# The first loads of `a` issued ahead of ScalarE's function table, with a new order of the whole program

## The chip, the cores and the metric

The kernel runs on one core of a Trainium2 chip. The time is device microseconds of one execution of the program; a kernel's time is the median of its runs. Beside the timed runs there is one profiled execution, whose trace is what the views below are read from. In the trace PE is TensorE (its weight loads stand apart as PEld), DVE is VectorE, ACT is ScalarE, POOL is GpSimd and SP is SyncE, and a name with a q behind it (ACTq, SPq) is that engine's sequencer issuing a DMA.

## The reference

A gated linear recurrence over 768 positions for 4 x 8 heads of width 48, with a complex decay per position, followed by a two-layer network with a squared ReLU:

```python
mag = np.sqrt(a_re * a_re + a_im * a_im)
scale = np.minimum(mag, 0.999) / (mag + 1e-06)
a_re_n, a_im_n = (a_re * scale, a_im * scale)
for t in range(S):
    S_re, S_im = a[t] * S (complex) + k[t] v[t]^T (into S_re)
    y[:, :, t] = q[:, :, t] @ S_re
x = y as (4*768, 384)
h = x @ w_in                       # 384 -> 2048
g = np.maximum(h, 0.0) ** 2
out = g @ w_out                    # 2048 -> 384, float32
```

## The kernel before

The 3072 tokens are cut into six units of 512. Each unit n goes through the same stations. Its `a`, `q`, `k`, `v` are loaded (`load`). `chain` turns `a` into running products: square roots by Ln and Exp on ACT with products on DVE (`roots`, `raw_products`, `normalise`), then two PE transposes of the totals (L1162 with `perm`; in unit 0 `joint`, L1183), copies to `e` on ACT (L1194, L1197), a scan of small products on DVE (L1283 to L1353, which writes `xn`), two transposes back (L1162 with `ident`), and the application to q and k (`apply`, L1422 to L1450). `pairs` then takes the eight heads two at a time: scores on PE (L1589), masks on DVE (L1595), states on PE and DVE (L1619, L1634), mix on PE (L1647, L1651), a copy to `yt` on ACT (L1657) and DMAs into `xT` (L1665). `dense` multiplies `xT` by `w_in` (L1707), ACT applies the squared ReLU (L1739, L1740), and the second product follows (L1754 in unit 0, L1908 from unit 1 on, where sums of blocks replace one product in eight; L1800 and L1908 in the last unit). In unit 0 there is also the conversion of the weights: each of 16 pieces is fetched by POOL (L833), scaled by ACT (L846, L847) and put together on DVE (L849, L852).

All of this is a list of steps handed to a planner (`Plan`): each step has an engine, an assumed duration, what it reads and writes, and a rank. The planner runs a list schedule over the assumed durations: the engine that is free first takes, of its steps that are ready, the one with the lowest rank. The order in which they come out is the order of the instructions on each engine. While PE would stand idle in it, the planner puts in multiplications of the identity by itself (L751), which nothing reads. Ranks are made from the station and the unit, and then shifted by a table of numbers, for groups of steps and for single steps:

```python
rank = 100 * s[4][0] + s[4][1] + groups.get(g, 0) + single.get(n, 0)
...
n = min((n for n in wait[e] if at[n] <= t), key=lambda n: (steps[n][4], n))
```

In unit 0 the loads of `a` come in three parts for each of the real and the imaginary half: two of four heads' halves (z = 0) and one of the other four heads (z = 1). SP issues the real parts and ACT the imaginary ones:

```python
queue = pool if n or half else act if j else sp
```

The function table is asked for in the program's first lines, ahead of every planned step (L673), and two small negations that ACT makes for PE (L1141) and the squares of the real part (L992) come behind it on ACT. POOL issues the loads of q and k, of v and of the weights behind two copies (L945) that wait for the two halves of `a`.

Of the kernel before, what the change touches and what calls it, by code (L numbers as in the profile page):

```python
# [638 lines left out]
def fast_path(ctx, tc, q, k, v, a_re, a_im, moe_w_in, moe_w_out, out, flag, ots, blocks_of):  # L639
# [28 lines left out]
    dve, pool, act, sp = nc.vector, nc.gpsimd, nc.scalar, nc.sync  # L668
# [1 line left out]

    const = ctx.enter_context(tc.tile_pool(name="const", bufs=1))
    psum = ctx.enter_context(tc.tile_pool(name="psum", bufs=1, space=PSUM))
    act.preload_act_table_set("natural_log_exp_and_others")  # L673

    def sb(name, n, dtype=F32, rows=C):
        return const.tile([rows, n], dtype, name=name)
# [36 lines left out]
                                                           r=2, b=2)  # L713
# [41 lines left out]
    def vs(n):  # L755
        return n % 2 if n < ROOM else 0

    def tt(n):
        return n / 960.0 + 0.07
# [4 lines left out]
    def ac(n):  # L764
        return n / 1200.0 + 0.18
# [3 lines left out]
    def step(*args, **kw):  # L769
        return plan.add(*args, **kw)  # L770
# [4 lines left out]
    def dma(q, reads, writes, fn, rank, size, lat=1.8, group=None, dur=None):  # L775
        name, took = ("POOL", 0.67) if q is pool else ("SP", 0.62) if q is sp else ("ACT", 0.6)
        step(name, dur or took, reads, writes, fn, rank, (lat, size), group)

    CHAIN, PAIR, DENSE, CONV, LATE = 2, 1, 3, 3, 5
# [114 lines left out]
    def parts(n):  # L894

        t, got = n * L, []
        while t < (n + 1) * L:
            b, s = divmod(t, S)
            m = min(S - s, (n + 1) * L - t)
            got.append(((t - n * L) // W, m // W, b, s))  # L900
            t += m
        return got

    def spans(i):

        return ((0, C, 0),) if i % 2 == 0 else ((C // 2, C, 0), (0, C // 2, C // 2))

    def load(n):
        rank = (CHAIN, n)
        for half, name, pair in ((0, "a", (a_re, a_im)), (1, "qk", (q, k))):  # L910
            for z in range(2):
                t = aq[z][:, half * Z:(half + 1) * Z].rearrange(
                    "p (r h x) -> p r h x", r=2, h=HH)
                late = []
                if half and n == 1:
                    late = [("gate", 0)]
                if half and n > 2:
                    late = [("xT", (n - 1) % 2, NM - 1)]
                if half and n == 0:
                    late = [("gate",)]  # L920

                if n == 1 and half == 0:
                    late = [("gk", z)]
                    step("POOL", 0.3, [(k_, z, 1) for k_ in ("KC", "KC0", "KC1")], late,
                         lambda z=z: pool.tensor_copy(
                             out=gate[:, 0:W - 1], in_=KC[z].rearrange(
                                 "p (i y x) -> p i y x", i=W, x=KW)[:, 1:W, 1, 0]), rank)

                cut = 2 if n == 0 and half == 0 and z == 0 else 1
                for u in range(cut):  # L930
                    for j, ap in enumerate(pair):
                        for p0, m, b, s in parts(n):
                            hs = slice(u * HH // cut, (u + 1) * HH // cut)
                            src = ap[b, z * HH + hs.start:z * HH + hs.stop, s:s + m * W, :]
                            src = src.rearrange("h (p c) d -> p h (c d)", c=W)
                            queue = pool if n or half else act if j else sp
                            dma(queue, late,
                                [(name, z)] + ([(name, z, "r", j, u)] if n == 0 else []),
                                lambda t=t, p0=p0, m=m, j=j, src=src, queue=queue, hs=hs:
                                queue.dma_start(out=t[p0:p0 + m, j, hs], in_=src),  # L940
                                rank, m * 3072 // cut, 5.0 if n else 3.0, group=n)
            if n == 0 and half == 0:
                for z in range(2):
                    step("POOL", 0.2, [("a", z)], [("gate",)],
                         lambda z=z: pool.tensor_copy(out=gate[:, z:z + 1],  # L945
                                                      in_=aq[z][:, Z - 1:Z]), rank)
        t = vv[vs(n)].rearrange("p (i h d) -> p i h d", i=W, h=H)
        for i in range(W):
            b, s = divmod(n * L + i * C, S)
            vrank = (CHAIN, 1) if n == 1 else (DENSE, 6 + n)  # L950
            for lo, hi, at in spans(i):
                src = v[b, :, s + at:s + at + hi - lo, :].rearrange("h p d -> p h d")
                dma(pool, [("gate", 0)] * (n == 1) + [
                    ("xT", (n - (vs(n) == vs(n - 1))) % 2, NM - 1)] if n else [("gate",)],
                    [("v", vs(n))], lambda i=i, lo=lo, hi=hi, src=src: pool.dma_start(
                        out=t[lo:hi, i], in_=src), vrank, (hi - lo) * 1536, 4.0, group=n)

    def chain(n):
        rank = (CHAIN, n)
# [15 lines left out]
        def roots(z):  # L975
# [5 lines left out]
            cut = 2 if n == 0 and z == 0 else 1  # L981
            size = Y // cut
            for u in range(cut):
                def k(*js, u=u):
                    return key(z, *js) if n else [("f", z, j, u) for j in js]
# [2 lines left out]
                    return x[:, ts(u, size)]  # L988
                if n == 0:

                    step("ACT", ac(size), [("a", z, "r", 0, u)], k(0),
                         lambda u=u: act.activation(  # L992
                             out=part(f0, u), in_=A[z][:, ts(u, size)], func=AF.Square), first)

                    def square(u=u):
                        x = A[z][:, Y + u * size:Y + (u + 1) * size]
                        dve.tensor_tensor(out=part(f1, u), in0=x, in1=x, op=ALU.mult)
                    step("DVE", tt(size), [("a", z, "r", 1, u)], k(1), square, first)
# [138 lines left out]
        K = [(k_, 0, q_) for k_ in ("KC", "KC0", "KC1") for q_ in range(2)]  # L1137
        nperm, minus = (yts[i][:, 0:C] for i in range(2))
        if n == 0:
            for i, by in ((1, ident), (0, perm)):  # L1140
                step("ACT", 0.25, [], [("yt", i)], lambda i=i, by=by: act.mul(  # L1141
                    out=yts[i][:, 0:C], in_=by, mul=-1.0), rank)
            for z in range(2):
                roots(z)
                raw_products(z)
# [914 lines left out]
    for n in range(AFTER):  # L2060
        for j in range(3):
# [1 line left out]
    verdict()  # L2063

    plan.shift(
        groups={11: -1.01, 12: 6.22, 13: 0.95, 15: 438.73, 16: 438.73, 17: -235.2, 20: 1.52, 72:
# [5 lines left out]
        single={19: -99.45, 23: -302.38, 32: 6.69, 37: 19.99, 41: 15.87, 42: 425.47, 44: 16.14, 67:  # L2072
# [14 lines left out]
    with tc.manual_schedule():  # L2087
        got = plan.emit(flag[0:1, 0:1])
    return got
# [59 lines left out]
```

## Time and profile before

| what | us |
|---|---|
| three runs, median (lowest to highest) | 656.53 (653.69 to 657.35) |
| profiled execution, whole | 657.09 |
| its span, first to last instruction | 655.3 |
| PE busy in the span | 641.8 (98%) |
| DVE busy | 574.8 (88%) |
| ACT busy | 379.3 (58%) |
| POOL busy | 150.0 (23%) |

The 657.09 of the profiled execution hold its span and 1.8 us around it. Busy time counts the filling multiplications too (L751, 45.5 us, nearly all in the first 60 us), so PE's share says little about the beginning; there the chain of work that ended last runs over DVE, and later over PE.

### The profile page before, as it was taken

How to read it: one execution, taken by the hardware profiler on the slowest of the kernel's cores; microseconds unless marked ns; L12 is line 12 of the kernel's file. 1: busy time of each engine (PE TensorE's matmuls, PEld its weight loads, DVE VectorE, ACT ScalarE, POOL GpSimd, SP SyncE). 2: the span in 40 equal slices, each digit the busy share in tenths (PEclk: the TensorE clock that was granted, in tenths of full speed). 3: DMA queues.
4: the chain of work that ended last, by engine and by line, in shares of the span. 5: the costliest groups of instructions: out<-in, count | busy, mean ns of one | idle time of the engine just before them, and what ended most of it. 6: DMA issues, size and time to landing. Idle time of an engine off the chain costs nothing.

```text
span 655.3 us, 13462 instructions
## 1 busy us (share of the span) xinstructions
PE 641.8 (98%) x5064; PEld 576.7 (88%) x5064; DVE 574.8 (88%) x1188; ACT 379.3 (58%) x651; POOL 150.0 (23%) x258
## 2 busy tenths in 40 slices
PE   8989999999999999999999999999999999999996
PEld 8978887687778988998989998989999989988996
DVE  6999999999799999988998997996978999379991
ACT  6999589975656356457356648057558164145500
POOL 7311543232200031042052052130050210022110
PEclk9999999999999999999999999999999999999999
DMA  6951679147810146433175344174270152258541
GB/s 208 352 165 43 149 181 303 33 106 186 222 49 2 37 109 147 108 96 99 48 176 130 80 113 97 27 196 115 52 181 26 38 143 62 62 198 262 191 169 31
DMA packets 34631, 81.80 MB, mean 125 GB/s; under 512 B 7894, under 2 KB 13411, under 8 KB 34556
## 3 DMA queue, kind: packets, MB, share of 16 engines
q0 software_dynamic: 17024, 58.60, 31.9%
q1 hardware_dynamic: 15356, 20.04, 11.9%
q10 hardware_dynamic: 2176, 2.20, 1.2%
q8 instruction: 42, 0.69, 0.5%
q14 instruction: 33, 0.27, 0.1%
HBM read 48.76 MB, written 4.72 MB: 82 GB/s over the span
## 4 chain that ended last, share of the span: by engine, by line
PE 69%; DVE 19%; DMA 5%; issue 3%; ACT 2%; SPq 1%; POOL 0%; DVEq 0%; ACTq 0%; POOLq 0%
PE d L1908 26%; PE d L1707 24%; PE sc L1589 3%; PE yp L1647 2%; PE d L1800 2%; PE d L1754 2%; PE yp L1651 2%; DVE f L1450 2%; PE tr L1619 2%; DMA aq<-in_a_im_dram 2%; PE tr L1800 2%; DVE f L1422 1%; PE sc L1800 1%; DMA e<-xn 1%; DMA xT<-yt 1%
## 5 line engine op out<-in xcount | busy, mean ns | idle before, releaser
L1707 PE MATMUL d<-xT,w 128*128 128x256 f32 x912 | 204.6, 380 | 0.7 <-DMA xT<-yt 0.6
L1707 PEld LDWEIGHTS d<-xT,w 128*128 128x128 f32 x912 | 171.4, 190 | 25.4 <-DMA xT<-yt 1.0
L1908 PE MATMUL d<-w,g 128*128 128x192 f32 x576 | 99.7, 326 | 0.0
L1739 ACT ACTIVATE g<-d 128x512 f32<-128x512 f32 x76 | 45.1, 594 | 87.6 <-PE d L1707 85.7
L1908 PEld LDWEIGHTS d<-w,g 128*128 128x128 f32 x576 | 94.5, 190 | 0.6
L1908 PE MATMUL d<-T,g 128*128 128x192 f32 x432 | 78.0, 329 | 0.3 <-DVE g L1922 0.3
L1908 PEld LDWEIGHTS d<-T,g 128*128 128x128 f32 x432 | 70.9, 190 | 1.9 <-DVE g L1922 0.8
L1864 POOL DMA_DIRECT2D out_dram<-ot x22 | 12.8, 580 | 202.3 <-DVE ot L1931 163.4
L1922 DVE TENSOR_TENSOR g<-g 128x512 f32<-128x512 f32 x72 | 48.5, 686 | 9.2 <-PE d L1908 4.6
L1496 POOL DMA_DIRECT2D KC<-f x56 | 34.7, 625 | 77.9 <-issue 44.8
L1740 ACT ACTIVATE g<-g 128x512 f32<-128x512 f32 x80 | 50.5, 632 | 2.6
L1539 ACT COPY QT<-aq 32x512 f32<-32x512 f32 x57 | 35.3, 619 | 23.7 <-DVE aq L1536 23.0
L1536 DVE STREAM_TRANSPOSE aq<-f 128x768 f32<-128x768 f32 x40 | 47.9, 1272 | 0.2
L1657 ACT COPY yt<-yp 112x512 f32<-112x512 f32 x24 | 26.6, 1107 | 36.1 <-PE yp L1651 36.1
L751 PEld LDWEIGHTS d<-ident 128*128 128x128 f32 x366 | 44.7, 202 | 3.1 <-POOL ident masks.py:199 1.6
L751 PE MATMUL d<-ident 128*128 128x128 f32 x366 | 45.5, 287 | 1.6 <-POOL ident masks.py:199 1.6
L1450 DVE TENSOR_TENSOR f<-aq 128x768 f32<-128x768 f32 (+1 forms) x56 | 44.3, 838 | 0.5
L1754 PE MATMUL d<-w,g 128*128 128x384 f32 x128 | 43.8, 490 | 0.0
L1589 PEld LDWEIGHTS sc<-QT 96*64 96x64 f32 x736 | 34.6, 137 | 3.5 <-issue 2.5
L1589 PE MATMUL sc<-QT 96*64 96x128 f32 (+1 forms) x736 | 36.8, 251 | 0.8 <-DVE A L1595 0.7
L1754 PEld LDWEIGHTS d<-w,g 128*128 128x128 f32 x128 | 23.8, 190 | 14.6 <-issue 0.4
L1931 DVE TENSOR_TENSOR ot<-ot,d 128x192 f32<-128x192 f32 x70 | 23.6, 349 | 14.4 <-PE d L1908 10.8
(274 smaller groups left out, 1170.6 us busy)
## 6 DMA issues: line engine op xcount, KB each, us to landing
QT<-aq SPq DMA_DIRECT2D x152, 64.0 KB
f<-in_moe_w_in_dram POOLq DMA_DIRECT2D x8, 768.0 KB, 6.1
f<-in_moe_w_out_dram POOLq DMA_DIRECT2D x8, 768.0 KB, 4.9
out_dram<-ot POOLq DMA_DIRECT2D x22, 192.0 KB, 2.2
KC<-f POOLq DMA_DIRECT2D x20, 192.0 KB, 4.4
xT<-yt SPq DMA_DIRECT2D x36, 96.0 KB
aq<-in_q_dram POOLq DMA_DIRECT2D x8, 384.0 KB, 5.4
aq<-in_k_dram POOLq DMA_DIRECT2D x8, 384.0 KB, 6.3
```

Of the source, the lines that this page charges most:

```text
L751: plan = Plan(lambda b: pe.matmul(bank[b][:, 0:C], lhsT=ident, rhs=ident, start=True, stop=True), ["d2", "d1", "d0"], lambda ap: tc.nc.val ...
L1450: lambda j=j, r=r, o=o: dve.tensor_tensor(out=o[:, :, :, r * D:(r + 1) * D], in0=qk[:, j], in1=a[:, r], op=ALU.mult), late[z])
L1496: lambda i=i, queue=queue, lo=lo, hi=hi, a0=a0, a1=a1: queue.dma_start(out=kc[lo:hi, i], in_=nat[a0:a1]),
L1536: lambda nat=nat, dst=dst, j=j: dve.transpose(out=dst[:, j], in_=nat), rank)
L1539: lambda b=b, t=t, T6=T6: act.copy(out=t[32 * b:32 * b + 32, b], in_=T6[32 * b:32 * b + 32, i % 2, b]),
L1589: pe.matmul(sa[r:r + C // 2, j, :, lo:32], lhsT=T[:, j, 1, h, ts(late, C // 2)], rhs=T[:, j, 0, h].rearrange("p (c t) -> p c t", c=W)[:, : ...
L1707: pe.matmul(ps, lhsT=w1[:, f // FP, m, ts(f % FP, C)], rhs=xT[:, n % 2, m, ts(grp, G)], start=(m == 0), stop=(m == NM - 1))
L1739: act.activation(out=o, in_=ps, func=AF.Relu)
L1740: act.activation(out=o, in_=o, func=AF.Square)
L1754: pe.matmul(ps, lhsT=gt[:, f % 2, ts(i, C)], rhs=w2[:, f], start=(f == 0), stop=(f == NF - 1))
L1908: pe.matmul(bank[b][:, 0:DH], lhsT=gs(r, h)[:, j - 4 * h], rhs=w(j), start=first and j == 0, stop=last and j == NT - 1)
L1922: step("DVE", tt(4 * C), gk(x0, h) + gk(x1, h), gk(o, h), lambda: dve.tensor_tensor(out=gs(o, h), in0=gs(x0, h), in1=gs(x1, h), op=op), (0 ...
```

## The change

The table load leaves the program's head and becomes a planned step of ACT with an assumed 1.28 us; the two negations and the squares of unit 0 read its key, so they come behind it, and the loads of `a`, which do not read it, come ahead. The assumed time from the issue to the landing of the first parts of `a` (z = 0 and z = 1, real and imaginary) goes from 3.0 to 2.0 us. The table of shifts is another one: 38 groups and 92 single steps before, 30 and 77 after, with hardly a number in common. The order of all engines was worked out anew with it; apart from the filling multiplications, of which there are four fewer, both kernels hold the same instructions.

```diff
-    act.preload_act_table_set("natural_log_exp_and_others")
...
                                 queue.dma_start(out=t[p0:p0 + m, j, hs], in_=src),
-                                rank, m * 3072 // cut, 5.0 if n else 3.0, group=n)
+                                rank, m * 3072 // cut, 5.0 if n else 2.0 if half == 0 else 3.0,
+                                group=n)
...
-                    step("ACT", ac(size), [("a", z, "r", 0, u)], k(0),
+                    step("ACT", ac(size), [("a", z, "r", 0, u), ("table",)], k(0),
                          lambda u=u: act.activation(
                              out=part(f0, u), in_=A[z][:, ts(u, size)], func=AF.Square), first)
...
         if n == 0:
+            step("ACT", 1.28, [], [("table",)], lambda: act.preload_act_table_set(
+                "natural_log_exp_and_others"), (CHAIN, 0.001))
             for i, by in ((1, ident), (0, perm)):
-                step("ACT", 0.25, [], [("yt", i)], lambda i=i, by=by: act.mul(
+                step("ACT", 0.25, [("table",)], [("yt", i)], lambda i=i, by=by: act.mul(
                     out=yts[i][:, 0:C], in_=by, mul=-1.0), rank)
...
     plan.shift(
-        groups={11: -1.01, 12: 6.22, 13: 0.95, 15: 438.73, 16: 438.73, 17: -235.2, 20: 1.52, 72:
...
+        groups={4: -101.6, 15: 450.38, 16: 451.94, 19: -213.0, 30: -204.21, 97: -103.99, 108: 0.71,
...
```

In the rows of the order below, the lines of the new kernel stand one lower than before between L674 and L938, the same up to L1137, and two higher from L1143 on (L1164 is what L1162 was, L1597 what L1595 was); the numbers behind the names of tiles are one lower (those of `d` excepted). The banks are `d_64` to `d_66`, `sc`, `tr` and `yp`.

ScalarE's first instructions before:

```order
L673 ACT_TABLE_LOAD
L1141 ACTIVATE yt_98<-ident 128x128
L1141 ACTIVATE yt_97<-perm 128x128
L940 DMA aq_76<-in_a_im_dram 128x2x192 x2
L940 DMA aq_77<-in_a_im_dram 128x4x192
L992 ACTIVATE f_78<-aq_76 128x384 x2
```

and now:

```order
L939 DMA aq_75<-in_a_im_dram 128x2x192 x2
L939 DMA aq_76<-in_a_im_dram 128x4x192
L1140 ACT_TABLE_LOAD
L1143 ACTIVATE yt_97<-ident 128x128
L1143 ACTIVATE yt_96<-perm 128x128
L992 ACTIVATE f_77<-aq_75 128x384
```

The three loads of the imaginary part stand first; the table load and what needs it follow.

VectorE at the end of unit 0's heads, from the masks of the third pair on, before:

```order
L1595 TENSOR_TENSOR A_93<-sc_113,mask 128x512
L1595 TENSOR_TENSOR A_94<-sc_114,mask 128x512
L852 ISA w_74<-w_75,w_74 128x1536
L849 TENSOR_SCALAR w_75<-w_75 128x768
L1000 TENSOR_TENSOR f_78<-f_78 128x768
L852 ISA w_75<-w_75 128x1536
L1634 TENSOR_TENSOR St_96<-tr_115,St_96 96x96 x2
L1634 TENSOR_TENSOR S_92<-tr_115,St_96 96x96
L1595 TENSOR_TENSOR A_93<-sc_113,mask 128x512
L1595 TENSOR_TENSOR A_94<-sc_114,mask 128x512
```

and now:

```order
L851 ISA w_73<-g,w_73 128x1536
L1636 TENSOR_TENSOR St_94<-tr_115,St_94 96x96 x2
L1636 TENSOR_TENSOR S_91<-tr_115,St_94 96x96
L851 ISA w_73<-w_74,w_73 128x1536
L848 TENSOR_SCALAR w_74<-T 128x768
L851 ISA w_74<-T,w_74 128x1536
L848 TENSOR_SCALAR w_73<-w_74 128x768
L1000 TENSOR_TENSOR f_77<-f_77 128x768
L1597 TENSOR_TENSOR A_92<-sc_112,mask 128x512
L1597 TENSOR_TENSOR A_93<-sc_113,mask 128x512
L851 ISA w_73<-w_74,w_73 128x1536
L1636 TENSOR_TENSOR St_95<-tr_114,St_95 96x96 x2
```

The last pair's states (L1634, now L1636) stood ahead of its masks and now stand behind them and behind one conversion; the third pair's states stood ahead of its masks too and now stand behind them (the first rows of the second piece).

TensorE in the last unit between the transposes of the totals (with `perm`) and the transposes back (with `ident`), before:

```order
L1162 MATMUL tr_115<-perm,xn 128x16x8 x3
L1707 MATMUL d_65<-xT,w_74 128x256 x3
L1707 MATMUL d_66<-xT,w_74 128x256 x6
L1707 MATMUL d_64<-xT,w_74 128x256 x6
L1707 MATMUL d_65<-xT,w_74 128x256 x6
L1707 MATMUL d_66<-xT,w_74 128x256 x6
L1707 MATMUL d_64<-xT,w_74 128x256 x6
L1908 MATMUL d_65<-w_75,g 128x192 x4
L1162 MATMUL tr_116<-ident,xn 128x128 x3
L1162 MATMUL tr_115<-ident,xn 128x128 x3
```

and now:

```order
L1164 MATMUL tr_114<-perm,xn 128x16x8 x3
L1709 MATMUL d_64<-xT,w_73 128x256 x6
L1709 MATMUL d_66<-xT,w_73 128x256 x3
L1709 MATMUL d_65<-xT,w_73 128x256 x3
L1709 MATMUL d_64<-xT,w_73 128x256 x6
L1709 MATMUL d_65<-xT,w_73 128x256 x3
L1709 MATMUL d_66<-xT,w_73 128x256 x6
L1709 MATMUL d_64<-xT,w_73 128x256 x3
L1164 MATMUL tr_115<-ident,xn 128x128 x3
L1164 MATMUL tr_114<-ident,xn 128x128 x3
```

Three products of L1707 and four of L1908 fewer now stand between the two.

More of the change, by code (lines that the diff above doesn't have):

```diff
@@ L2065, in fast_path @@
     plan.shift(
-        groups={11: -1.01, 12: 6.22, 13: 0.95, 15: 438.73, 16: 438.73, 17: -235.2, 20: 1.52, 72:
[5 rows of a table removed]
-        single={19: -99.45, 23: -302.38, 32: 6.69, 37: 19.99, 41: 15.87, 42: 425.47, 44: 16.14, 67:
[14 rows of a table removed]
+        groups={4: -101.6, 15: 450.38, 16: 451.94, 19: -213.0, 30: -204.21, 97: -103.99, 108: 0.71,
[4 rows of a table added]
+        single={11: -0.81, 12: 103.36, 16: 98.42, 17: 98.35, 25: 1.5, 37: 19.35, 40: 23.91, 49:
[12 rows of a table added]
     with tc.manual_schedule():
```

35 rows, old and new, of tables (groups, single) are left out of this document.

## The prediction

> **What bounds the kernel now.** I read the chain that ended last first, in order of time: start, length, what. Of its first 90 us these pieces matter here.
>
> ```profile
> 0.82 1.28 ACT L673
> 2.27 4.14 DMA aq<-in_a_im_dram
> ...
> 10.94 0.88 DVE f L997
> 11.91 0.96 DVE f L1000
> ...
> 82.26 1.07 ACT yt L1657
> 83.36 4.53 DMA xT<-yt
> 88.21 2.40 PE d L1707 x10
> ```
>
> The program begins with the table load, the transfer of the imaginary part of `a` stands behind it, and from there the chain runs over VectorE until the third pair of heads of unit 0 is copied to `yt`, sent to `xT`, and TensorE can begin the dense work at 88.21. The table by stretches shows who is full in each (length, then PE, PEld, DVE, ACT and POOL busy, the clock, the DMA engines' share and GB/s).
>
> ```profile
> 6.44:80.00 73.56, 68.97 (x753) 63.11 (x753) 71.52 (x185) 61.00 (x94) 27.71 (x46) 1.00 0.62 180
> 88.20:212.00 123.80, 122.65 (x769) 95.19 (x770) 114.78 (x239) 93.26 (x157) 32.66 (x50) 1.00 0.50 131
> 212.30:650.10 437.80, 437.44 (x3419) 406.63 (x3417) 379.30 (x750) 215.44 (x386) 84.88 (x133) 1.00 0.41 112
> ```
>
> Up to 80 us DVE is busy 71.52 of 73.56 us: what starts it earlier, or takes work from it, moves the dense start. From 88.2 on PE has work nearly all the time (122.65 of 123.80, 437.44 of 437.80), and the work is the same in both kernels. So the time is the dense start, plus PE's work behind it, plus PE's waits. A wait of PE there is short now:
>
> ```profile
> PE tr L1162 <- DVE xn L1353: 0.6, 1, 0.6
> PE d L1707 <- DMA xT<-yt: 0.6, 1, 0.6
> PE yp L1647 <- ACT yt L1657: 0.5, 1, 0.5
> PE d L1908 <- DVE g L1922: 0.3, 1, 0.3
> ```
>
> These waits after 88 us add to 2.0 us, which is the most that a better order can win behind the dense start.
>
> **Part one: the loads of `a` go ahead of the table.** The timeline of the first microseconds (start, length, engine, line, what; in brackets the idle time before):
>
> ```profile
> 0.82 1.48 SPq L940 DMA_DIRECT2D aq<-in_a_re_dram  x3
> 2.11 0.31 ACT L1141 ACTIVATE yt<-ident 128x128 f32<-128x128 f32 x1
> 2.27 0.43 ACTq L940 DMA_DIRECT2D aq<-in_a_im_dram  x1
> 2.33 0.29 ACT L1141 ACTIVATE yt<-perm 128x128 f32<-128x128 f32 x1
> 2.73 1.00 ACTq L940 DMA_DIRECT2D aq<-in_a_im_dram  x2
> 3.79 0.94 ACT L992 ACTIVATE f<-aq 128x384 f32<-128x384 f32 x2 [1.16 <-DMA aq<-in_a_re_dram]
> 6.44 0.56 DVE L997 TENSOR_TENSOR f<-aq 128x384 f32<-128x384 f32 x1 [4.95 <-DMA aq<-in_a_im_dram]
> 7.38 0.55 DVE L1000 TENSOR_TENSOR f<-f 128x384 f32<-128x384 f32 x1
> ```
>
> ACT can begin at 0.82, where its table load begins now, so the first imaginary part is issued at 0.82 instead of 2.27, beside SP's real parts. It lands at the earliest as SP's first part does, 3.79 - 0.82 = 2.97 us after its issue, at 3.79, and at the latest with its own time of now, 4.14 us, at 4.96. The bandwidth says where between:
>
> ```profile
> 1.00:2.00 1.00, 0.35 (x1) 0.35 (x2) 0.48 (x1) 1.00 (x1) 0.96 (x5) 1.00 0.08 8
> 3.50:4.00 0.50, 0.50 (x5) 0.50 (x4) 0.00 (x0) 0.21 (x1) 0.50 (x9) 1.00 0.51 86
> 8.00:8.50 0.50, 0.50 (x7) 0.50 (x6) 0.50 (x2) 0.49 (x1) 0.00 (x0) 1.00 0.00 0
> ```
>
> The DMA engines drop to half (0.51, 86 GB/s) between the real and the imaginary parts. With both in flight this hole closes, but the two first parts share the engines. I take the middle, 4.4, so that DVE starts 2.0 us earlier (1.5 to 2.7). The Trainium skill, DMA: Bandwidth & Descriptors, section Issuing engines are not separate DMA queues, speaks against even that: DMAs issued by several engines run on the same 16 DMA engines and interleave, and issuing on several at once only saves sequencer time, "which is usually small relative to the DMA itself". By this the saving would be as good as none; here the sequencer's time is 1.45 us of a wait of 4.95, and the hole of the row above is not the engines' limit.
>
> ACT pays: three issues (0.43 + 1.00), then the load (1.28), then two negations at 0.22 from start to start, so its first square starts at 0.82 + 1.43 + 1.28 + 0.44 = 3.97 instead of 3.79 and ends by 4.5 (half of 0.94). DVE's L1000 waits for that square and for its own L997 (4.4 to 4.9), so ACT does not cap the gain: L1000 at 4.9 against 7.38. If the landing came at 3.79, ACT would be late next, with 4.5, and 0.2 us of the 2.7 would be lost.
>
> The Trainium skill, ScalarE: Activation LUTs, section What ACT_TABLE_LOAD costs, adds a drain of about 1.38 us to a load of 1.283. By that estimate L1000 would come at 5.9 and the gain be 1.5 us. The load's 1.28 agrees; the drain does not, since the first negation follows at 2.11, 0.01 us after the load's end.
>
> **Part two: VectorE's work ahead of the dense start.** The dense start waits for the third pair. Counted over both orders, the same DVE instructions stand ahead of the third mix, except one L849 fewer now. The fourth pair's three L1634 move behind its masks, with one L852 between. Their durations:
>
> ```profile
> L852 DVE CUSTOM_DVE_ANT_0 w<-w,w 128x1536 uint16<-128x1536 uint16 x3 | 2.8, 948 | 0.0
> L849 DVE TENSOR_SCALAR w<-T 128x768 uint32<-128x768 uint32 x3 | 1.7, 554 | 0.0
> L1634 DVE TENSOR_TENSOR St<-tr,St 96x96 f32<-96x96 f32 x6 | 1.5, 250 | 0.1
> 83.00 1.27 DVE L1595 TENSOR_TENSOR A<-sc,mask 128x512 f32<-128x512 f32 x2
> 86.11 1.12 ACT L1657 COPY yt<-yp 112x512 f32<-112x512 f32 x1 [1.17 <-PE yp L1651]
> ```
>
> One L849 fewer gives 0.5 us (0 to 0.55). So by the third pair the dense start is at 88.21 - 2.0 - 0.5 = 85.7. The fourth pair must not be later, because its mix now stands right ahead of the dense work: its masks end at 84.27 - 2.0 - 3 x 0.25 = 81.5, then come L852 (0.95), three L1634 (0.75) and the mix (about 1.8, from the masks' end at 84.27 to the copy at 86.11): 85.0. That is hidden behind the third pair by 0.7 us; if the cover went, each microsecond of lateness would cost one.
>
> **Part three: the order behind the dense start.** Every unit's transposes back on PE follow the scan's last instruction on DVE closely. In the last unit:
>
> ```profile
> 485.94 0.66 PE tr L1162 x6
> 486.60 14.25 PE d L1707 x66
> 500.85 1.30 PE d L1908 x8
> 502.15 0.66 PE tr L1162 x6
> ```
>
> ```profile
> 487.93 0.60 ACT L1739 ACTIVATE g<-d 128x512 f32<-128x512 f32 x1
> 488.56 0.63 ACT L1740 ACTIVATE g<-g 128x512 f32<-128x512 f32 x1
> 489.10 0.39 ACT L1197 ACTIVATE e<-tr 128x288 f32<-128x288 f32 x1
> 500.89 0.65 DVE L1353 TENSOR_TENSOR xn<-KC 128x288 f32<-128x288 f32 x1
> ```
>
> L1353 ends at 501.54 and its transposes start at 502.15. Now 6 of the 66 passes of L1707 (6 x 14.25/66 = 1.3 us) and the 8 of L1908 (1.3) no longer stand between, so PE arrives 2.6 us earlier. On ACT the pair of L1739 and L1740 moves behind L1197, which frees the scan 1.2 us earlier; with the 0.6 of slack 0.8 us of wait is left, unless the scan starts earlier for another reason. In units 2, 3 and 4 the first of these transposes comes 0.9, 1.3 and 0.4 us of PE's work earlier. In unit 2 four L1127 and two L1134 move on DVE from ahead of the scan to behind it while two L1893 come ahead, which lets that scan end earlier as well. The bounds are therefore all of today's waits gone (a gain of 2.0) and all shorter covers paid, 0.9 + 1.3 + 0.4 + 2.6 = 5.2 us. I take a loss of 0.5, near the rows of now, where these waits are 0.6 at most.
>
> **Sum.** -2.0 - 0.5 + 0.5 = -2.0 us. From the profiled execution's own 657.09 (span 655.3 and 1.8 around it) that is 655.1; the median of the runs lies 0.56 lower, which gives 654.5. I name 654.8. A difference of 0.5%, 3.3 us, is about what a measurement of this kernel can tell from no change.
>
> **Rivals.**
> *A, slower: the transposes back wait for the scans.* Place: L1162 with `ident` in units 2 to 5. PE is the bound there, so a wait is not made up. Price: 5.2 us if no scan gets shorter, hence 657.09 - 2.5 + 5.2 = 659.8, and it makes the kernel slower as soon as more than 2.5 us of it show. For it: 2.6 us in the last unit against 0.6 of slack. Against it: L1197 is freed by 1.2 in the same place.
> *B, no head start.* The two halves of `a` interleave, the real part lands later by what the imaginary one wins, and DVE starts at 6.4 as now, or the loads behind (q, k, weights) keep the later chain where it is. Only the 0.5 of the L849 stays, against the 0.5 lost: 656.5 to 657.1. For it: the skill's rule on issuing engines. Against it: the half-empty row at 3.5.
> *C, faster.* Head start at its bound, 2.7 - 0.2, the 0.5, and nearly all of today's 2.0 us of waits gone: 657.09 - 5.0 = 652.1. For it: the order frees L1197 and unit 2's scan, places at which the trace shows a delay. Against it: an order can hardly meet every wait at once.
> That the change does not do what it says is excluded by ScalarE's order: the three loads do stand first.
>
> **Chances and range.** Forecast 0.46, A 0.16, B 0.16, C 0.22. The range reaches from C (652.1, and 0.56 lower by the median: 651.5) to just short of A's full price: 659.3. Faster by over 0.5% (under 653.2) takes C and 0.04 of the forecast: 0.26. Slower by over 0.5% (over 659.8) takes nearly A's full price or a wait that I did not see: 0.14. Within 0.5%: 0.60.
>
> **What would show it.** Right: DVE's L997 starts at 4.4 (1.5 to 2.7 us earlier), L1707 starts steadily near 85.7, and the last multiplication ends about 2 us earlier. Part one is wrong if L997 starts at 6 or later; part two if L1707 waits for the fourth pair; part three if the waits of L1162 for L1353 add to over 2 us. The whole is wrong if a wait of PE that is absent now, above all for a transfer, takes more than 3 us.

## The result and the profile after

The changed kernel takes 656.83 us (median of 21 runs, 654.88 to 660.28), the kernel before 655.74 us (21 runs, 653.54 to 658.59). The ratio is 1.0028, 95% interval [1.0016, 1.0040]: 1 to 2.6 us slower, where 2 us faster was forecast. That is less than the 0.5% that the prediction took for the limit of a measurement; 21 runs of each resolve it. The profiled execution of the changed kernel took 660.28 us (span 658.5), the longest of its runs, and that of before 657.09, 1.35 above its median. So sizes are read from a second trace of the changed kernel too (657.23, span 655.4), and what decides is the timed ratios. The ratios and their intervals, here and below, are estimates that come with the measurement; the quotient of the two medians differs from them by up to 0.1% (here it is 1.0017).

The start, in the timeline of the changed kernel (start, length, engine, line, what; in brackets the idle time before):

```profile
0.83 1.54 ACTq L939 DMA_DIRECT2D aq<-in_a_im_dram  x3
2.40 1.28 ACT L1140 ACT_TABLE_LOAD   x1 [2.40 <-issue]
4.30 0.56 DVE L997 TENSOR_TENSOR f<-aq 128x384 f32<-128x384 f32 x1 [2.81 <-DMA aq<-in_a_im_dram]
8.69 0.96 DVE L997 TENSOR_TENSOR f<-aq 128x768 f32<-128x768 f32 x1 [0.77 <-DMA aq<-in_a_im_dram]
```

The head start is there: VectorE begins at 4.30 instead of 6.44. But it meets the second half of `a` too early now and waits 0.77 us for it. Further on, from the timelines of TensorE and VectorE:

```profile
77.57 0.40 PE L1621 MATMUL tr<-v,KC 128*64 128x48 f32 x8 [1.77 <-DMA KC<-f]
78.34 0.54 DVE L1636 TENSOR_TENSOR St<-tr,St 96x96 f32<-96x96 f32 x2 [1.23 <-ACT St L1629]
79.84 0.65 PE L1649 MATMUL yp<-A,v 128*48 128x128 f32 x8
83.77 2.27 PE L750 MATMUL d<-ident 128*128 128x128 f32 x18
85.12 0.53 DVE L1636 TENSOR_TENSOR St<-tr,St 96x96 f32<-96x96 f32 x2
85.97 0.65 PE L1649 MATMUL yp<-A,v 128*48 128x128 f32 x8
87.65 2.86 PE L1709 MATMUL d<-xT,w 128*128 128x256 f32 x12
```

The kernel before has at the same places:

```profile
79.92 0.60 PE L1647 MATMUL yp<-A,v 128*48 128x128 f32 x7
87.00 0.60 PE L1707 MATMUL d<-xT,w 128*128 128x256 f32 x2
88.21 2.40 PE L1707 MATMUL d<-xT,w 128*128 128x256 f32 x10 [0.61 <-DMA xT<-yt]
```

The third pair's states wait for the transfer that lays out its `KC`. The third mix comes at 79.84, no earlier than before (79.81, and seven more products from 79.92), and the fourth, right ahead of the dense work, at 85.97. Between the third mix and the dense work TensorE is never idle: 18 filling multiplications stand ahead of the fourth mix. It takes 7.81 us from the one to the other in both traces of the changed kernel and 7.19 before, so what is late at the third mix is late at the dense work. The dense work begins at 87.65. Before, it began at 87.00, did two products, waited 0.61 and went on at 88.21: of the head start nothing is left at the first product, and 0.56 us where the work goes on steadily. VectorE's row in the table by stretches says where it went. The stretch runs from its first L997 to the end of the fourth pair's masks (length, then PE, PEld, DVE busy), first in the kernel before:

```profile
6.44:84.28 77.84, 73.25 (x820) 67.06 (x818) 75.70 (x194) 65.00 (x101) 29.24 (x48) 1.00 0.64 183
```

and in the changed kernel:

```profile
4.30:84.33 80.03, 73.64 (x815) 67.50 (x814) 75.56 (x191) 65.73 (x102) 33.10 (x48) 1.00 0.65 193
```

The work is the same to 0.14 us (75.70 and 75.56), the idle time grew from 2.14 to 4.47 (length less busy time). So: 2.14 earlier, 2.33 more idle, 0.14 less work, and 0.60 more between the masks' end and the first dense product (3.32 against 2.72): 87.65 against 87.00. The second trace gives the same sum with other terms: start 4.46, idle 3.69, dense work at 86.83.

Behind the dense start, TensorE's waits (line, what it waited for, us in all, times, longest) in the changed kernel:

```profile
PE tr L1164 <- DVE xn L1355: 1.6, 2, 1.2
PE yp L1649 <- ACT yt L1659: 1.5, 1, 1.5
PE d L1910 <- DVE ot L1933: 1.0, 1, 1.0
PE tr L1709 <- DVE w L851: 0.5, 1, 0.5
```

4.6 us instead of 2.0, and 4.3 in the second trace. From the first dense product to the end of the last multiplication it is 565.5 us (second trace 564.9) against 563.1 before.

### The profile page after: what moved, and what is told of

The parts are those of the page before. It is cut to its first block, busy times and chain, and to the rows that moved or that the text cites. A ratio compares the mean times of both kernels' runs of the same rounds, so it can differ in the third digit from the quotient of the medians.

```text
span 658.5 us, 13436 instructions
## 1 busy us (share of the span) xinstructions
PE 640.4 (97%) x5056; PEld 575.1 (87%) x5056; DVE 575.6 (87%) x1188; ACT 379.7 (58%) x651; POOL 154.0 (23%) x258
## 4 chain that ended last, share of the span: by engine, by line
PE 65%; DVE 17%; DMA 6%; ACT 6%; issue 3%; SPq 1%; POOL 1%; DVEq 0%; POOLq 0%; ACTq 0%
PE d L1910 26%; PE d L1709 20%; PE sc L1591 3%; PE d L750 3%; PE yp L1649 2%; PE d L1802 2%; DVE f L1452 2%; PE yp L1653 2%; PE tr L1621 2%; DMA QT<-aq 2%; PE tr L1802 2%; DMA T<-in_moe_w_out_dram 1%; DMA xT<-yt 1%; DVE KC L1305 1%; PE sc L1802 1%
## 5 line engine op out<-in xcount | busy, mean ns | idle before, releaser
L1910 PE MATMUL d<-w,g 128*128 128x192 f32 x576 | 100.1, 327 | 0.0
L1910 PEld LDWEIGHTS d<-w,g 128*128 128x128 f32 x576 | 94.5, 190 | 0.7
L1910 PE MATMUL d<-T,g 128*128 128x192 f32 x432 | 77.8, 328 | 1.0 <-DVE ot L1933 1.0
L1910 PEld LDWEIGHTS d<-T,g 128*128 128x128 f32 x432 | 71.0, 190 | 2.5 <-DVE ot L1933 1.3
L1924 DVE TENSOR_TENSOR g<-g 128x512 f32<-128x512 f32 x72 | 48.3, 684 | 5.9 <-PE d L1910 3.9
L1452 DVE TENSOR_TENSOR f<-aq 128x768 f32<-128x768 f32 (+1 forms) x56 | 44.0, 837 | 0.4
L1591 PE MATMUL sc<-QT 96*64 96x64 f32 (+1 forms) x736 | 38.4, 252 | 0.8 <-ACT QT L1572 0.8
L1933 DVE TENSOR_TENSOR ot<-ot,d 128x192 f32<-128x192 f32 x70 | 23.4, 347 | 13.1 <-PE d L1910 9.4
```

The costliest lines, as they stand in the source:

```text
L1452: lambda j=j, r=r, o=o: dve.tensor_tensor(out=o[:, :, :, r * D:(r + 1) * D], in0=qk[:, j], in1=a[:, r], op=ALU.mult), late[z])
L1591: pe.matmul(sa[r:r + C // 2, j, :, lo:32], lhsT=T[:, j, 1, h, ts(late, C // 2)], rhs=T[:, j, 0, h].rearrange("p (c t) -> p c t", c=W)[:, : ...
L1910: pe.matmul(bank[b][:, 0:DH], lhsT=gs(r, h)[:, j - 4 * h], rhs=w(j), start=first and j == 0, stop=last and j == NT - 1)
L1924: step("DVE", tt(4 * C), gk(x0, h) + gk(x1, h), gk(o, h), lambda: dve.tensor_tensor(out=gs(o, h), in0=gs(x0, h), in1=gs(x1, h), op=op), (0 ...
```

## The experiments

In all but the repeat of the changed kernel the order isn't planned: it is written out as the list of step numbers that the planner of the one or the other kernel gave, with its filling multiplications. "Old order" is that of before, "new order" that of the change; an edit moves the named steps and no others. Line numbers are those of the changed kernel. The edits show rows of the order.

**The change taken apart.** First the old order with the loads first:

```diff
+L939 DMA aq_75<-in_a_im_dram 128x2x192 x2
+L939 DMA aq_76<-in_a_im_dram 128x4x192
 L1140 ACT_TABLE_LOAD
 L1143 ACTIVATE yt_97<-ident 128x128
 L1143 ACTIVATE yt_96<-perm 128x128
-L939 DMA aq_75<-in_a_im_dram 128x2x192 x2
-L939 DMA aq_76<-in_a_im_dram 128x4x192
```

> The order of before, step for step, with one difference: ScalarE issues its three loads of a first and the table load follows. Theory G (the head start is real, the new order gives it back): L997 starts at 4.3 us as in the changed kernel, VectorE keeps at least 1.4 of the 2.1 us up to the third pair, the dense work starts steadily at 86.1 to 86.8 instead of 88.21, and the time is 1.4 to 2.1 us under before (653.6 to 654.3 if before stands at 655.7). Rival H (the head start is worth nothing by itself, since something later holds the first unit): L997 at 4.3 too, but dense start at 88 and the time of before, 655.7.

Measured: 653.0 us against 654.45, ratio 0.9977 [0.9965, 0.9989]. From the timelines of this kernel:

```profile
4.45 0.56 DVE L997 TENSOR_TENSOR f<-aq 128x384 f32<-128x384 f32 x1 [2.96 <-DMA aq<-in_a_im_dram]
77.60 0.60 PE L1649 MATMUL yp<-A,v 128*48 128x128 f32 x7
84.68 2.96 PE L1709 MATMUL d<-xT,w 128*128 128x256 f32 x12
```

and its stretch to the fourth masks:

```profile
4.45:81.96 77.51, 73.69 (x829) 67.76 (x828) 75.36 (x194) 65.66 (x103) 29.73 (x48) 1.00 0.67 194
```

VectorE starts 1.99 us earlier, its idle time is 2.15, as before, the third mix comes 2.3 earlier and the dense work too (84.68 against 87.00). In this order nothing eats the head start. Then the opposite, the new order with the table load and the negations ahead of the loads (the same rows, moved back):

> The order of the changed kernel, with the table load and the two negations put back ahead of ScalarE's three loads of a. G: L997 at 6.44 again; VectorE's wait of 0.8 us for the second half of a goes, so that some 1.4 us of the 2.1 are lost, dense start at 89.0 instead of 87.65, time 1.4 us above the changed kernel (658.2). H: dense start at 87.65 and the time of the changed kernel, 656.8.

Measured: 659.54 us, 1.0072 of before [1.0053, 1.0091], with

```profile
6.57 0.56 DVE L997 TENSOR_TENSOR f<-aq 128x384 f32<-128x384 f32 x1 [5.09 <-DMA aq<-in_a_im_dram]
88.94 2.88 PE L1709 MATMUL d<-xT,w 128*128 128x256 f32 x12
```

The trace is as expected (1.3 us later), the time a little more than that (0.44% over the changed kernel, 2.9 us). The two repeats:

> The old order with ScalarE's loads first, once more, as the kernel that the next three are compared with. G: 0.9977 of before, L997 near 4.45, VectorE without a wait from there to the third pair's masks, the third pair's mix at 77.6. The landing of the third pair's xT may differ from one execution to the next (it took 3.7 us in one trace, 6.2 us in the run with the new order behind), so the dense start lies between 84.7 and 87.5.

> The changed kernel itself once more, for a second trace and a time beside the next three. G: its trace has again a wait of TensorE for the third pair's KC ahead of the dense work, and behind it waits of L1164 in unit 2 (1.2 us) and of L1910 for L1933 (1.0 us); 1.0028 of before. If the later waits were this one execution's, they are under 0.6 us each here.

The old order with the loads first came to 653.83 us against 654.7, 0.9978 [0.9955, 1.0001]; the changed kernel to 656.94 against 655.24, 1.0021 [1.0004, 1.0038], with these waits behind the dense start:

```profile
PE tr L1164 <- DVE xn L1355: 1.6, 2, 1.2
PE yp L1649 <- ACT yt L1659: 1.2, 1, 1.2
PE d L1910 <- DVE ot L1933: 1.0, 1, 1.0
PE tr L1709 <- DVE w L851: 0.5, 1, 0.5
```

and this one ahead of it:

```profile
76.75 0.40 PE L1621 MATMUL tr<-v,KC 128*64 128x48 f32 x8 [0.34 <-DMA KC<-f]
```

So the later waits are not one execution's. The wait for `KC` was, in its size: 0.34 us instead of 1.77, with no wait of VectorE at the third pair's L1636, while the second half of `a` costs 1.31 instead of 0.77. In the second trace of the old order with the loads first the dense work begins at 85.19 and, after a pause of 0.94, goes on steadily from 86.72 (before: 87.00 and 88.21). Four corners, as ratios to before:

| | old order | new order |
|---|---|---|
| loads behind table and negations | 1 | 1.0072 |
| loads first | 0.9977, 0.9978 | 1.0028, 1.0021 |

The loads win 0.23% in the old order (1.5 us) and 0.44 to 0.51% in the new one; the new order loses 0.43 to 0.51% (about 3 us) with the loads first and 0.72% without.

**Which end of the new order.** Each of the two orders up to its first dense product, joined to the other behind it:

> The changed kernel's order for every step that it plans ahead of its first dense product, and the order of before for all steps behind. G, with the later waits as a part: dense start at 87.65, TensorE's waits behind it back at about 2.0 us from 4.6, time 1.1 to 2.6 us under the changed kernel (654.2 to 655.7). Rival (the loss lies ahead of the dense work, and the longer waits behind it are only this one profile's): the time of the changed kernel, 656.8.

> The order of before with ScalarE's loads first (as in the run with the old order) for every step that it plans ahead of its first dense product, and the changed kernel's order for all steps behind. G: L1709 begins near 84.7 as in that run, but the new order's waits behind cost about 2.4 us (its three traces have 564.8 to 565.4 us from the first dense product to the last multiplication, those of the old order 561.8 to 562.8), so 1.0013 of before. Rival (the later waits are not in the typical execution, the loss lies ahead of the dense work): 0.9977 as that run.

New, then old: 655.8 us, 1.0025 [1.0013, 1.0038]; the dense work begins at 87.22. Old, then new: 655.85 us, 1.0003 [0.9983, 1.0022], and the trace shows the transfer of the third pair late:

```profile
84.81 0.60 PE L1709 MATMUL d<-xT,w 128*128 128x256 f32 x2
87.48 3.39 PE L1709 MATMUL d<-xT,w 128*128 128x256 f32 x10 [2.07 <-DMA xT<-yt]
```

Measured from the old order with its loads first, the new beginning costs 0.48% and the new end 0.26%. Together that is more than the 0.43 to 0.51% of both at once. Measured from the changed kernel (1.0028 and 1.0021) instead, the old beginning wins 0.18 to 0.25% back and the old end nothing (1.0025), although TensorE's waits behind the dense start are down to 2.4 us in its trace. So the beginning loses on both readings; a loss by the end shows in the time only behind the old beginning, and the exact shares stay open. The first of the two expectations failed, since it put the loss behind the dense start.

**The places of the beginning.** The third pair's gathers, in the changed kernel's timeline of GpSimd:

```profile
65.88 2.99 POOL L924 COPY gate<-KC 128x3 f32<-128x3 f32 x1 [2.71 <-DMA KC<-f]
68.82 0.63 POOL L939 DMA_DIRECT2D aq<-in_a_re_dram  x1
69.44 1.57 POOL L1498 DMA_DIRECT2D KC<-f  x3
```

A gate that waits for other transfers, and a load for unit 1, stand ahead of them. The edit, on GpSimd (on SyncE likewise the gathers ahead of two L1667):

```diff
-L924 COPY gate<-KC_82 128x3
-L939 DMA aq_75<-in_a_re_dram 64x4x192
 L1498 DMA KC_83<-f_78 128x1x192
 L1498 DMA KC_83<-f_78 64x1x192 x2
+L924 COPY gate<-KC_82 128x3
+L939 DMA aq_75<-in_a_re_dram 64x4x192
```

> The changed kernel's order, with two moves: on GpSimd the gathers of the third pair's KC (three L1498) go ahead of the gate copy L924 and the one load of unit 1's a that stand before them now, and on SyncE the third pair's other gathers go ahead of the two xT transfers of the first pair. G: the third pair's KC lands about 2 us earlier, TensorE's wait of 1.8 us (L1621) and VectorE's of 1.2 us (L1636) go, dense start at 86.2 to 86.5 instead of 87.65, time 1.2 to 1.4 us under the changed kernel (655.5). Rival (the gathers are late because their transfers are slow among others, not because they are issued late): TensorE still waits over 1 us, dense start and time as in the changed kernel.

The trace does as expected: no wait for `KC`, third mix at 78.34, dense start at 86.14. The time doesn't show it: 656.32 us, 1.0027 [1.0009, 1.0045]. In the second trace of the changed kernel that wait is small as it is, and its dense work begins at 86.83, so about 0.7 us would be to be had in an execution like that one, less than the interval. The reverse, in the old order with the loads first (gate and load put ahead of the gathers):

> The old order with ScalarE's loads first, and on GpSimd the gate copy L924 and one load of unit 1's a put ahead of the third pair's gathers, as the new order has them. G: the gathers are issued about 2 us later, TensorE waits 1 to 2 us for the third pair's KC at L1621, the third mix comes at 78.6 to 79.6 instead of 77.6, and 1 to 1.5 us are lost: 0.9992 to 1.0000 of before. Rival (the old order has slack there, the late gathers cost nothing): third mix at 77.6, 0.9977.

The rival held: third mix at 78.02 (77.60 and 77.93 without the move), 652.81 us, 0.9963 [0.9946, 0.9981]. The gathers went out at 66.25, which is 1.2 to 1.5 us later (64.77 and 65.10) and not the 2 that were expected; for that much the old order has slack. The second half of `a`, met earlier in the old order with the loads first:

```diff
 L997 TENSOR_TENSOR f_77<-aq_75 128x384
+L997 TENSOR_TENSOR f_78<-aq_76 128x768
 L1032 TENSOR_TENSOR KC_82<-aq_75 128x2x192
 L1000 TENSOR_TENSOR f_77<-f_77 128x384
 L1010 SCALAR_TENSOR_TENSOR f_77<-f_77 128x384
-L997 TENSOR_TENSOR f_78<-aq_76 128x768
```

> The old order with ScalarE's loads first, and on VectorE the second half's L997 put ahead of one L1032, one L1000 and one L1010, so that it meets the landing of its half of a. G: VectorE waits 1.0 to 1.4 us there and is late by as much at the third mix (78.6 to 79.0); 1.0 to 1.4 us are lost: 0.9992 to 0.9998 of before. Rival (the start of the chain has slack, the wait is made up later): third mix at 77.6, 0.9977.

```profile
8.86 0.96 DVE L997 TENSOR_TENSOR f<-aq 128x768 f32<-128x768 f32 x1 [1.58 <-DMA aq<-in_a_im_dram]
79.65 0.60 PE L1649 MATMUL yp<-A,v 128*48 128x128 f32 x7
```

A wait of 1.58 us puts the third mix at 79.65 instead of 77.6 to 77.9: in this trace nothing makes it up. Not all of the wait is the edit's, since the half itself lands later here: GpSimd's gate (L945), which waits for it, comes at 8.89 and not at 8.00 as in the first run of this order. The time, 654.08 us, 0.9986 [0.9966, 1.0005], goes that way by 0.08%, within its interval.

**The places of the end.** Two moves on VectorE in the new order:

```diff
 L1895 TENSOR_TENSOR T<-w_74,T 128x768
-L1895 TENSOR_TENSOR T<-w_74 128x768
-L1895 TENSOR_TENSOR w_74<-w_74 128x4x192
 L1285 TENSOR_TENSOR KC_82<-e 128x192
...
-L1452 TENSOR_TENSOR f_77<-aq_75 128x4x4x48 x4
+L1452 TENSOR_TENSOR f_77<-aq_75 128x4x4x48 x3
 L1933 TENSOR_TENSOR ot_63<-ot_62,d_65 128x192
 L1933 TENSOR_TENSOR ot_63<-ot_63,d_64 128x192
+L1452 TENSOR_TENSOR f_77<-aq_75 128x4x4x48
```

(the two L1895 stand behind the scan's last L1355 then). The scan that they delay, and what waits for it in the changed kernel:

```profile
201.09 0.96 DVE L1895 TENSOR_TENSOR w<-w 128x768 f32<-128x768 f32 x1
201.97 0.35 DVE L1285 TENSOR_TENSOR KC<-e 128x192 f32<-128x192 f32 x1
212.97 0.52 PE L1164 MATMUL tr<-ident,xn 128*128 128x128 f32 x3 [1.18 <-DVE xn L1355]
```

> The changed kernel's order with two moves on VectorE behind the dense start: in unit 2 the last two L1895 ahead of the scan go behind it, and in unit 4 the first two of three L1933 go ahead of the last L1452. G: the waits of L1164 (1.2 us, to 0.5 or less) and of L1910 (1.0 us, to 0.3 or less) shrink, 1.4 us less than the changed kernel, 1.0006 of before. Rival (another wait takes their place): 1.0028.

> The same two moves, the two moves of the gathers on GpSimd and SyncE, and one more on VectorE at the start: the third of the four small L1032 products goes ahead of the second half's L997, into the 0.8 us in which VectorE waits for that half. G, if the named places are all of it: dense start 1.5 us (gathers) and 0.5 us (L1032) earlier, 1.4 us behind it, 3.4 us in all under the changed kernel, 0.9976 of before, level with the old order with its loads first. If something unnamed is left: over 0.9995.

The first took 655.93 us, 1.0013 [0.9991, 1.0035], which leaves both of its cases open. The second, which has all the moves together, took 657.06 us, 1.0021 [1.0003, 1.0038]: something that the named places don't hold is left. The waits of the first:

```profile
PE tr L1164 <- DVE xn L1355: 0.9, 2, 0.7
PE d L1910 <- DVE g L1924: 0.8, 2, 0.4
PE yp L1649 <- ACT yt L1659: 0.6, 1, 0.6
PE tr L1709 <- DVE w L851: 0.5, 1, 0.5
```

The wait for L1933 is gone; moving the L1895 shortened one wait by 0.7 us and made another of 0.8 just behind it, for sums (L1924) that now stand behind the L1895. In the run with all moves the extra L1032 also made a new wait, of 0.5 us at L1010. So the two good moves alone, gathers and L1933:

> The changed kernel's order with the gathers of the third pair put forward (as in the run with that alone) and, in unit 4, two of the three L1933 ahead of the last L1452; the L1895 stay where they are, since moving them made new waits of 0.8 us for L1924 behind the scan. G: VectorE's idle time ahead of the dense start falls by 0.9 to 1.3 us and TensorE's wait for L1933 (1.0) goes: 1.5 to 2.2 us under the changed kernel, 0.9990 to 1.0003 of before. If the loss is spread over places that no single wait shows: 1.0020 to 1.0028.

```profile
4.70:82.98 78.28, 73.67 (x818) 67.50 (x818) 75.53 (x191) 65.65 (x102) 30.10 (x48) 0.98 0.64 191
```

655.39 us against 655.02, 1.0002 [0.9993, 1.0011]: 1.2 to 1.7 us of the loss come back, with VectorE's idle time at 2.75 and the dense start at 85.73. The interval lies under that of the changed kernel's 21 runs, though not under that of its repeat. That these two places held the lost time is likely and not shown: in this trace the second half of `a` cost no wait either, which neither move touches. In the second trace of the changed kernel that wait is 1.31 us, and the idle time fell by less, from 3.69 to 2.75. The rest, 0.25% over the old order with the loads first, is not accounted for one by one.

The granted clock differs between the beginnings as well, and no run varied it by itself. In the row above it is 0.98, since TensorE was granted half its clock from 39.8 to 43.2 us. Six of the eight traces with the new beginning have such a stretch of 3.4 us between 38 and 48 us, and none of the eight with the old beginning has one there. Of the timed executions, 67 of 99 with the new beginning have a mean clock of 0.997 or less, and 18 of 192 with the old one (the kernel before included). In each kernel with the new beginning these have a median 0.3 to 2.2 us above that of the others. It is not the whole loss: among the others alone the repeat of the changed kernel is at 1.0022 of before (7 executions against 32). Whether the new order brings this stretch about, and what part of the 0.25% it is, stays open.

**What held the loads.** Only the third load behind the table load and the negations, in the old order:

> The old order, with two of ScalarE's loads of a ahead of the table load and the third, for the second half, behind it and behind the two negations. G: that load is issued 1.4 us later and lands near 10.1 instead of 8.7; VectorE needs it at 8.9, waits 1.0 to 1.3 us for it, and as much is lost: 0.9992 to 0.9997 of before, so that the first two loads alone win 0.3 to 0.8 us. If the landing of the third load is set by the transfers and not by its issue: no wait, 0.9977.

```profile
0.83 1.02 ACTq L939 DMA_DIRECT2D aq<-in_a_im_dram  x2
1.88 1.28 ACT L1140 ACT_TABLE_LOAD   x1 [1.88 <-issue]
2.27 0.37 ACTq L939 DMA_DIRECT2D aq<-in_a_im_dram  x1
3.17 0.31 ACT L1143 ACTIVATE yt<-ident 128x128 f32<-128x128 f32 x1
```

653.53 us, 0.9975 [0.9954, 0.9995], and no wait; but the expected late issue didn't happen either. The third load went out at 2.27, in the middle of the table load. 2.27 is also when the loads began in the kernel before. GpSimd's row in this trace:

```profile
1.82 0.41 POOL L726 COPY perm<-ident 128x128 f32<-128x128 f32 x1
```

Its end, 2.23, is what the second negation waits for. So in the last kernel the order is table load, loads, negations.

> The old order with the table load first again, then the three loads of a, then the two negations. In the traces so far the loads that stand behind the negations begin at 2.27 us whether the table load ends at 2.10 or (in the run with only the third load behind) at 3.16, and GpSimd's copy of perm, which the second negation reads, ends at 2.23 in each. N (the loads were held by the negation that waits for GpSimd): they are issued before the table load is over, near 0.9, L997 starts at 4.3 to 4.7, and the time is that of the loads standing first, 0.9978 of before. T (the table load holds them, as the change's own words have it): issue at 2.1, L997 at 6.3, 0.9995 to 1.0 of before.

```profile
0.82 1.28 ACT L1140 ACT_TABLE_LOAD   x1 [0.82 <-PEq L2132]
0.86 1.52 ACTq L939 DMA_DIRECT2D aq<-in_a_im_dram  x3
2.43 0.31 ACT L1143 ACTIVATE yt<-ident 128x128 f32<-128x128 f32 x1 [0.33 <-POOL mask L731]
4.59 0.56 DVE L997 TENSOR_TENSOR f<-aq 128x384 f32<-128x384 f32 x1 [3.10 <-DMA aq<-in_a_im_dram]
```

The case N held. The loads go out while the table is loaded, VectorE starts at 4.59, and the kernel takes 652.21 us against 655.02, 0.9955 [0.9942, 0.9968]: the best of all, under both kernels of the change. It was the negations that held the loads, not the table load; that it was their wait for GpSimd's copy is read from the times (2.23 and 2.27 in the kernel before and in two of the runs), since no run moved the copy itself. Whether it really beats the order with the loads first (0.9977, 0.9978) the intervals don't settle.

## Why the prediction was wrong

**Part one, the head start: right in size, wrong in cause.** L997 was forecast at 4.4 and came at 4.30, L1000 at 4.9 and came at 4.97. The sentence that the transfer stands behind the table load named the wrong instruction: the trace of before had the sign, a load issued at 2.27 when the table load had ended at 2.10, and GpSimd's copy would have explained the difference. By the Trainium skill, DMA: Bandwidth & Descriptors, section Issuing engines are not separate DMA queues, issuing on several engines at once saves only the time of issuing, which is usually small beside the transfer. What the change took away was a wait and not that time: the loads go out 1.44 us earlier, VectorE starts 2.0 us earlier, and 0.23% of the time is won.

**Part two, "VectorE's work ahead of the dense start": the step that failed.** The instructions were counted right: from the first L997 to the third mix VectorE has one L849 fewer and is busy 71.22 us (70.93 in the second trace) instead of 71.33, so that this gave 0.1 to 0.4 us and not 0.5. What was taken for granted was that VectorE would be as free of waits in the new order as in the old. Up to the fourth masks it idled 2.33 us more in the one trace and 1.55 in the other: 0.77 and 1.31 at the second half of `a`, 1.23 and nothing at the third pair's states, the rest in smaller pieces. So the dense start forecast for 85.7 came at 87.65 and 86.83. The old order with its loads first, in which VectorE's idle time stayed what it was (2.15 and 2.14), does what the step said, to within the wait for a transfer: 84.68 without a wait in one trace, steadily from 86.72 in the other. The step also took the dense start from the third pair's transfer into `xT`. In the changed kernel TensorE doesn't wait for it: it works without a break from the third mix through the fourth to the dense work. The cover of 0.7 us for the fourth pair doesn't exist in such an order, and the masks' end and the dense start lie 0.60 further apart. It is not the place of the fourth pair's states that makes these 0.60: with the third pair's gathers put forward and VectorE's order as it was, they don't appear (2.75 instead of 3.32).

**Part three, the order behind the dense start: a term mis-sized.** 0.5 us of loss was taken; the traces have 1.8 to 2.4, and the two joined orders give 0.26% (1.7 us) behind the old beginning and nothing that can be told behind the new one. Rival A had the mechanism in part: L1164 waits 1.6 us instead of 0.6, in units 2 and 4. In the last unit, where it saw 2.6 us at stake, there is no wait. The other new waits were in none of the steps: L1910 for a sum that VectorE does behind four L1452 (1.0), and L1649 for a copy that ScalarE does late (1.2 to 1.5 instead of 0.5; from none to 1.0 in the traces of the runs that have this end behind another beginning or with moves).

**The rivals.** B is out: the head start exists. C assumed that an order could only take waits away. A was priced too high at its place and missed the others. The outcome is a mixture for which no case stood: a real gain at the head, consumed within 80 us by waits of VectorE, and a smaller loss behind, which the time shows less surely.

## What to carry to other kernels

When an edit comes with a new order, price the two apart: here the edit alone won 0.23% and the order lost twice that. A head start on a busy engine arrives only as far as nothing on its way waits for a transfer that didn't move; so list, along the chain, the landings that stay where they are, and how much slack each has. And where an instruction is held, look at which of the instructions ahead of it on its engine has a semaphore to wait for, before blaming the longest one.

## What the runs showed of the hardware

A DMA issue on ScalarE went out at 0.86 and 2.27 us while a table load of 1.28 us was running (0.82 to 2.10, 1.88 to 3.16), so a table load doesn't hold back the issues behind it. Behind the negations, the second of which waits for a copy that GpSimd ends at 2.23, the issue went out at 2.27 whether the table load ended at 2.10 or at 3.16. With a first ACTIVATE 0.01 us behind the table load (3.68 and 3.69 in the changed kernel) no drain is seen; the Trainium skill, ScalarE: Activation LUTs, section What ACT_TABLE_LOAD costs, gives one of about 1.38 us for a switch. The transfer of the third pair's `xT`, issued at 81.04 us, let the dense work go on without a wait in one execution of the old order with its loads first (84.68); in another with the same order ahead of it, issued at 81.16, it took 6.05 us and held the work for 2.07 us (87.48). In the kernel before it took 4.53 us, and the wait was 0.61. Between these executions a transfer alone moves the steady start of the dense work by as much as the change moves the time.
